# The last four rows of an output projection, summed in four rows of 256 columns or in two rows of 512

## The chip, the cores and the metric

The kernel runs on one core of one Trainium2 chip. The core has engines with an instruction stream each: TensorE (PE in the profile; its weight loads have a row of their own, PEld), VectorE (DVE), ScalarE (ACT), GpSimd (POOL) and SyncE (SP), which here only issues transfers. Sixteen DMA engines move data between device memory and the on-chip memories. The matmuls write to PSUM, everything else lives in SBUF. The metric is the device time of one execution in microseconds; of several executions the median is given.

## The reference

One token goes through two branches that share a layer norm, and both are added to the input. The attention branch uses the last 4,096 positions of the caches, 32 query heads over 4 key/value heads.

```python
xn = layernorm(x)                        # x: 1 x 1024
q = xn @ wq                              # 32 heads of 128
k, v = k_cache[-4096:], v_cache[-4096:]  # 4 heads, each serves 8 query heads
o = softmax(q @ k.T * 128 ** -0.5) @ v   # 1 x 4096
h = gelu(layernorm(xn) @ w1 + b1)        # 1 x 3584
out = x + o @ wo + h @ w2 + b2           # wo: 4096 x 1024, w2: 3584 x 1024
```

The result is one row of 1,024 numbers in bfloat16.

## The kernel before

All work is a chain of vector-matrix products, so nearly every byte that is read is used once: 4 MB each of keys, values and wq, twice 3.5 MB of w1 and of w2, and twice 4 MB of wo. The large tiles go through a ring of four SBUF buffers (`ring`, line 54); a load into a buffer has to wait until its last user is done. SP issues the loads in the order of the program: keys, wq, w1, values, w2, wo.

VectorE transposes the keys (line 186), VectorE and ScalarE spread them out (lines 200 and 202), TensorE makes q (line 238), the hidden layer (line 258), the scores (line 276) and the attention output (line 320). A few small tensors are made at the start by GpSimd: `spread` (lines 108 to 111) and `gmask` (lines 113 to 118), which are needed much later, and the two reciprocal square roots of the layer norms (lines 145 and 168). VectorE works on the layer norms meanwhile; `xc` (line 135) and `xn_f` (line 146) are two of its small steps.

The last stage is the sum over w2 and wo. `chunk_src` lists 28 rows of w2 and 32 of wo; a row is a [128, 1024] slab, and its product with one column of `hT` or `o8` gives a share of the 1,024 outputs. A matmul takes the one column as its stationary operand and up to 512 columns of the slab as its moving operand, and writes one PSUM partition. `tile_position=(0, 32 * half)` places the two halves of 512 columns in PSUM partitions 0 and 32. All rows but the last four go into the PSUM tile `accf` (line 341), which already holds x + b2.

The second wo tile is loaded in pieces of 8, 4, 2, 1 and 1 rows (line 227), so that the last rows arrive in small pieces; a matmul waits for the piece with its row. The last four rows (`TAIL = 4`) are rows 13 to 16 of that tile. They go into two PSUM tiles of their own, `acct`: the first holds columns 0 to 319 of each half and is finished by VectorE, the second columns 320 to 511, finished by ScalarE (`N1 = 320`). While the last rows arrive, `accf` is copied out to `bulk`: ScalarE copies 192 columns of both halves (line 345), VectorE 320 (line 346). ScalarE's share is added by TensorE, with the identity as stationary operand (line 353), so that ScalarE need only copy the result at the end (line 362); VectorE adds its share itself (line 361):

```python
    nc.vector.tensor_tensor(out=res[:, 0:N1], in0=acct[0][0:33, :], in1=bulk[0][:], op=ALU.add)
    nc.scalar.copy(out=res[:, N1:512], in_=acct[1][0:33, :])
    nc.sync.dma_start(out=out_v[0:1, :], in_=res[0:1, :])
    nc.scalar.dma_start(out=out_v[1:2, :], in_=res[32:33, :])
```

`res` has one half of the output in partition 0 and the other in partition 32; the partitions between are carried along. SP stores the first half and ScalarE the second, and each store needs both engines' columns.

Of the kernel before, what the change touches and what calls it, by code (L numbers as in the profile page):

```python
# [8 lines left out]
FP32 = mybir.dt.float32  # L9
BF16 = mybir.dt.bfloat16  # L10
ACT = mybir.ActivationFunctionType
ALU = mybir.AluOpType
# [4 lines left out]
def kernel(  # L17
# [14 lines left out]
    nc = tc.nc  # L32
# [21 lines left out]
    consts = ctx.enter_context(tc.tile_pool(name="consts", bufs=1))  # L54
# [8 lines left out]
    def ring_tile(name):  # L63
        return ring.tile([P, RING_ELEMS], BF16, tag="ring", name=name, align_bytes=256)
# [13 lines left out]
    for i in range(2):  # L78
        t = ring_tile(f"wq{i}")
# [8 lines left out]
    ident_f = consts.tile([P, P], FP32)  # L88
# [12 lines left out]
    with tc.issue_after(first_exp.ins):  # L101
# [8 lines left out]
    nc.gpsimd.affine_select(out=spread[:], in_=spread[:], compare_op=ALU.not_equal, fill=1.0, base=0,  # L110
                            pattern=[[-1, 4], [1, P]], channel_multiplier=-4)

    gmask = consts.tile([Hq, Hkv], FP32)
    nc.gpsimd.memset(gmask[:], 1.0)
    nc.gpsimd.affine_select(out=gmask[:], in_=gmask[:], compare_op=ALU.is_ge, fill=0.0, base=0,
# [56 lines left out]
    accf = ps_acc.tile([P, 512], FP32, tag="accf")  # L172
# [3 lines left out]
    for half in range(2):  # L176
        pr = 32 * half
        nc.tensor.matmul(accf[pr:pr + 1, :], lhsT=ones_bf[0:2, 0:1], rhs=xb2[:, 512 * half:512 * half + 512],
                         start=True, stop=False, tile_position=(0, pr))
# [24 lines left out]
    for i in range(2):  # L204
        t = ring_tile(f"w1{i}")
# [11 lines left out]
    for i in range(2):  # L217
        nr = CW2 // 2
        t = ring_tile(f"w2{i}")
# [4 lines left out]
    for i, cuts in enumerate([[0, 16], [0, 8, 12, 14, 15, 16]]):  # L224
        nr = CWO // 2
        t = ring_tile(f"wo{i}")
# [6 lines left out]
    for i, w3 in enumerate(wq_tiles):  # L233
        for r in range(4):
            c = 4 * i + r
            for j in range(NJQ):
                b, t = divmod(j, 4)
                nc.tensor.matmul(accq[32 * t:32 * t + 1, b, :], lhsT=xnT[:, c:c + 1], rhs=w3[:, r, j * 512:(j + 1) * 512],  # L238
                                 start=(c == 0), stop=(c == C - 1), tile_position=(0, 32 * t))
# [8 lines left out]
    for j in range(8):  # L248
        t, b = divmod(j, 2)
        nc.tensor.matmul(acch[32 * t:32 * t + 1, b, :NH], lhsT=ones_bf[0:1, 0:1], rhs=b1_row[:, j * NH:(j + 1) * NH],  # L250
                         start=True, stop=False, tile_position=(0, 32 * t))
    for i, w3 in enumerate(w1_tiles):
        for r in range(4):
            c = 4 * i + r
            for b in range(2):
                for t in range(4):
                    j = 2 * t + b
                    nc.tensor.matmul(acch[32 * t:32 * t + 1, b, :NH], lhsT=yT[:, c:c + 1], rhs=w3[:, r, j * NH:(j + 1) * NH],  # L258
                                     start=False, stop=(c == C - 1), tile_position=(0, 32 * t))
# [3 lines left out]
    for g in range(Hkv):  # L263
        b, th = divmod(g, 2)
# [6 lines left out]
    for a in range(WQ4 // 512):  # L271
        sp = ps_f.tile([P, 512], FP32, tag="pf", name="sp")
        for R in range(4):
            for g in range(Hkv):
                c0 = WQ4 * R + 512 * a
                nc.tensor.matmul(sp[32 * R:32 * R + 32, :], lhsT=qm[:, g, :], rhs=kT[:, g, c0:c0 + 512],  # L276
                                 start=(g == 0), stop=(g == Hkv - 1), tile_position=(0, 32 * R))
# [41 lines left out]
    for c in range(NCH):  # L319
        nc.tensor.matmul(o_all[:].rearrange("h g d -> h (g d)"), lhsT=eTb[:, 32 * c:32 * c + 32], rhs=v4[:, :, c, :],  # L320
                         start=(c == 0), stop=(c == NCH - 1))
# [11 lines left out]


    vec = {"h": lambda c: hT[:, c, 0:1], "o": lambda c: o8[:, c:c + 1]}
    N1 = 320
    TAIL = 4
    n_bulk = len(chunk_src) - TAIL
    for idx, (kind, c, wap) in enumerate(chunk_src[:n_bulk]):
        for half in range(2):  # L340
            nc.tensor.matmul(accf[32 * half:32 * half + 1, :], lhsT=vec[kind](c), rhs=wap[:, half * 512:(half + 1) * 512],  # L341
                             start=False, stop=(idx == n_bulk - 1), tile_position=(0, 32 * half))
    cols = ((0, N1), (N1, 512))
    bulk = [consts.tile([33, b - a], FP32, name=f"bulk{i}") for i, (a, b) in enumerate(cols)]
    nc.scalar.copy(out=bulk[1][:], in_=accf[0:33, N1:512])  # L345
    nc.vector.tensor_copy(out=bulk[0][:], in_=accf[0:33, 0:N1])  # L346
    acct = [ps_f.tile([P, b - a], FP32, tag="pf", name=f"acct{i}") for i, (a, b) in enumerate(cols)]
    for t in acct:
        nc.vector.memset(t[0:33, :], 0.0)
    for idx, (kind, c, wap) in enumerate(chunk_src[n_bulk:]):  # L350
        if idx == TAIL - 2:
            for half in range(2):
                nc.tensor.matmul(acct[1][32 * half:32 * half + 1, :], lhsT=ident_f[0:33, 32 * half:32 * half + 1], rhs=bulk[1][:],
                                 start=False, stop=False, tile_position=(0, 32 * half))
        for t, (n0, n1) in zip(acct, cols):
            for half in range(2):
                nc.tensor.matmul(t[32 * half:32 * half + 1, :], lhsT=vec[kind](c),  # L357
                                 rhs=wap[:, half * 512 + n0:half * 512 + n1],
                                 start=(idx == 0), stop=(idx == TAIL - 1), tile_position=(0, 32 * half))
    res = consts.tile([33, 512], BF16)  # L360
    nc.vector.tensor_tensor(out=res[:, 0:N1], in0=acct[0][0:33, :], in1=bulk[0][:], op=ALU.add)
    nc.scalar.copy(out=res[:, N1:512], in_=acct[1][0:33, :])
    out_v = out.rearrange("a b (t n) -> (a b t) n", t=2)
    nc.sync.dma_start(out=out_v[0:1, :], in_=res[0:1, :])
    nc.scalar.dma_start(out=out_v[1:2, :], in_=res[32:33, :])


# [28 lines left out]
```

## Time and profile before

| what | before |
|---|---|
| time, median of 3 runs | 101.66 us (101.6, 101.66, 101.79) |
| span of the profiled execution, first to last instruction | 100.03 us (100.0 on the page) |
| loaded from device memory | 39.86 MB, 398 GB/s over the span |
| TensorE busy | 51.2 us (51%) |
| VectorE busy | 49.7 us (50%) |
| ScalarE busy | 34.1 us (34%) |
| GpSimd busy | 3.8 us (4%) |
| mean granted TensorE clock | 0.778; 1.00 from 95 us on |

The profile shows one execution; its own whole time is not listed apart from the three runs, and 101.66 − 100.03 = 1.63 us of the median lie outside the span.

How to read its views. In the view of slices the span is cut into 40 equal parts, and each digit is the busy share of a part in tenths (9 is 90% or more). The chain that ended last is followed back from the last instruction: each step is what released the next one, or the instruction before it on its engine. A line of the timeline gives start and length in microseconds, engine, line of the code, operation, the tile written and those read, and the shape; in brackets stands how long the engine was idle before and what ended that. Neighbouring instructions of one line are merged there ("x4"), and the merged line is named after its first. The groups by form list the same operations by shape: the total busy time, then the mean of one in nanoseconds, then the idle time of the engine ahead of them. "PEq" and "SPq" are the engines' instruction sequencers.

### The profile page before, as it was taken

The page shows a single profiled execution, that of the slowest core. Times are in us where ns is not written, and L with a number is a line of the kernel's source. Part 1 is how long each engine was busy: PE and PEld are TensorE (multiplying, and loading weights), DVE is VectorE, ACT ScalarE, POOL GpSimd, SP SyncE. Part 2 cuts the span into 40 slices and gives each one's busy share as a digit, 9 for nine tenths or more (in the row PEclk, how much of TensorE's full clock was granted, in tenths as well). Part 3 has the DMA queues.
Part 4 walks back from the last instruction along what each step waited for, and adds up shares of the span by engine and source line. Part 5 has one row for each costly group of instructions (what it writes and reads, how often), then busy time and mean ns, then how long its engine had stood idle before and what let it go on. Part 6 is the DMA issues. An engine that isn't in the chain of part 4 may idle for free.

```text
span 100.0 us, 970 instructions
## 1 busy us (share of the span) xinstructions
PE 51.2 (51%) x365; PEld 20.0 (20%) x365; DVE 49.7 (50%) x92; ACT 34.1 (34%) x37; POOL 3.8 (4%) x16
## 2 busy tenths in 40 slices
PE   0065200008500940193892935999469950199980
PEld 0042200002100310031530322334123410033320
DVE  5445499999999999997125115410450000000021
ACT  5000002999999999962001044400000000000010
POOL 6005200000000000000000000000000000000000
PEclk9999999999995579555555555559985998557999
DMA  2999999999999999998999999999999999999920
GB/s 26 394 420 426 491 488 472 419 419 419 432 419 393 401 500 382 413 482 378 390 429 426 429 531 390 413 477 390 459 447 426 419 432 419 406 419 411 401 73 1
DMA packets 2878, 39.92 MB, mean 399 GB/s; under 512 B 309, under 2 KB 311, under 8 KB 698
## 3 DMA queue, kind: packets, MB, share of 16 engines
q1 hardware_dynamic: 2866, 39.85, 93.6%
q8 instruction: 3, 0.05, 0.2%
q10 hardware_dynamic: 8, 0.01, 0.0%
q14 instruction: 1, 0.01, 0.0%
HBM read 39.86 MB, written 0.00 MB: 398 GB/s over the span
## 4 chain that ended last, share of the span: by engine, by line
DVE 38%; DMA 24%; PE 21%; issue 9%; POOL 3%; ACT 2%; SPq 1%; POOLq 1%; ACTq 0%
DMA wo<-in_A_wo_dram 24%; DVE kt_scr L186 17%; DVE kT L202 16%; PE o_all L320 10%; PE sp L276 4%; PE acch L258 3%; ACT e L298 1%; DVE eTb L300 1%; PE qT_ps L262 1%; DVE m_loc L284 1%; PE acct L357 1%; SPq L229 1%; DVE q_sb L241 1%; POOLq L391 1%; POOL spread L110 1%
## 5 line engine op out<-in xcount | busy, mean ns | idle before, releaser
L200 ACT COPY kT<-kt_scr 32x1024 bf16<-32x1024 bf16 x26 | 27.1, 1042 | 14.8 <-DVE kt_scr L186 14.5
L186 DVE STREAM_TRANSPOSE kt_scr<-k_sb 128x4096 bf16<-128x4096 bf16 x4 | 17.4, 4411 | 0.0
L238 PE MATMUL accq<-wq,xnT 128*1 128x512 bf16 x64 | 7.1, 622 | 18.3 <-DMA wq<-in_A_wq_dram 18.3
L202 DVE COPY kT<-kt_scr 32x1024 bf16<-32x1024 bf16 x38 | 15.9, 419 | 0.5
L346 DVE COPY bulk<-accf 33x320 f32<-33x320 f32 x1 | 0.5, 483 | 21.9 <-ACT bulk L345 21.9
L341 PE MATMUL accf<-wo,o 128*1 128x512 bf16 x56 | 8.3, 459 | 6.0 <-DMA wo<-in_A_wo_dram 5.9
L345 ACT COPY bulk<-accf 33x192 f32<-33x192 f32 x1 | 0.3, 312 | 31.9 <-PE accf L341 31.9
L320 PE MATMUL o_all<-v_sb,eTb 128*32 128x512 bf16 x32 | 10.0, 491 | 1.0 <-DVE zcol L311 1.0
L258 PE MATMUL acch<-w,yT 128*1 128x448 bf16 x64 | 6.3, 572 | 6.0 <-DMA w<-in_B_w_dram 6.0
L341 PE MATMUL accf<-w,hT 128*1 128x512 bf16 x56 | 7.9, 451 | 0.0
L238 PEld LDWEIGHTS <-xnT 128*1 128x1 bf16 x64 | 2.1, 116 | 22.5 <-issue 22.4
L320 PEld LDWEIGHTS <-eTb 128*32 128x32 bf16 x32 | 3.8, 120 | 6.9 <-issue 3.9
L341 PEld LDWEIGHTS <-o 128*1 128x1 bf16 x56 | 2.8, 97 | 11.4 <-issue 9.2
L258 PEld LDWEIGHTS <-yT 128*1 128x1 bf16 x64 | 2.0, 115 | 9.8 <-issue 9.8
L276 PE MATMUL sp<-kT,qm 128*32 128x512 bf16 x32 | 3.8, 630 | 0.3 <-DVE qm L267 0.3
L341 PEld LDWEIGHTS <-hT 128*1 128x1 bf16 x56 | 2.7, 96 | 4.7 <-issue 2.5
L323 DVE TENSOR_TENSOR o_m<-o_all,grs 32x512 f32<-32x512 f32 x1 | 0.7, 680 | 5.8 <-PE o_all L320 5.8
L123 PE MATMUL x_ps<-ones_bf,xb 1*128 1x1 bf16 x8 | 0.7, 200 | 5.0 <-DMA xb<-in_A_x_dram 5.0
L298 ACT ACTIVATE e<-sc,nmx 128x1024 bf16<-128x1024 f32 x1 | 1.1, 1148 | 5.7 <-DVE nmx L295 5.7
L315 DVE STREAM_TRANSPOSE hT<-h_sb 128x896 bf16<-128x896 bf16 x1 | 1.7, 1706 | 2.4 <-ACT h_sb L313 2.4
L276 PEld LDWEIGHTS <-qm 128*32 128x32 bf16 x32 | 2.1, 133 | 1.4 <-issue 0.9
L281 ACT COPY sc<-sp 128x512 f32<-128x512 f32 x1 | 0.6, 585 | 4.8 <-PE sp L276 4.8
(88 smaller groups left out, 35.9 us busy)
## 6 DMA issues: line engine op xcount, KB each, us to landing
w<-in_B_w_dram SPq DMA_DIRECT2D x4, 3584.0 KB
wq<-in_A_wq_dram SPq DMA_DIRECT2D x2, 4096.0 KB, 27.0
k_sb<-in_A_k_cache_dram SPq DMA_DIRECT2D x4, 1024.0 KB, 7.1
wo<-in_A_wo_dram SPq DMA_DIRECT2D x1, 4096.0 KB, 29.4
v_sb<-in_A_v_cache_dram SPq DMA_DIRECT2D x1, 2048.0 KB, 19.2
v_sb<-in_A_v_cache_dram SPq DMA_DIRECT2D x2, 1024.0 KB, 23.1
wo<-in_A_wo_dram SPq DMA_DIRECT2D x1, 2048.0 KB
wo<-in_A_wo_dram SPq DMA_DIRECT2D x1, 1024.0 KB
```

Source lines behind the costliest of these rows:

```text
L110: nc.gpsimd.affine_select(out=spread[:], in_=spread[:], compare_op=ALU.not_equal, fill=1.0, base=0, pattern=[[-1, 4], [1, P]], channel_mul ...
L186: nc.vector.transpose(out=scr[:, g, :], in_=k2[:, g, :])
L200: nc.scalar.copy(out=dst, in_=src)
L202: nc.vector.tensor_copy(out=dst, in_=src)
L229: nc.sync.dma_start(out=tv[:, a:b, :], in_=wo_v[:, nr * i + a:nr * i + b, :])
L238: nc.tensor.matmul(accq[32 * t:32 * t + 1, b, :], lhsT=xnT[:, c:c + 1], rhs=w3[:, r, j * 512:(j + 1) * 512], start=(c == 0), stop=(c == C ...
L258: nc.tensor.matmul(acch[32 * t:32 * t + 1, b, :NH], lhsT=yT[:, c:c + 1], rhs=w3[:, r, j * NH:(j + 1) * NH], start=False, stop=(c == C - 1) ...
L276: nc.tensor.matmul(sp[32 * R:32 * R + 32, :], lhsT=qm[:, g, :], rhs=kT[:, g, c0:c0 + 512], start=(g == 0), stop=(g == Hkv - 1), tile_posit ...
L298: nc.scalar.activation(out=e128[:], in_=sc[:], func=ACT.Exp, bias=nmx[:], scale=scale, accum_out=l_loc[:])
L315: nc.vector.transpose(out=hT[:], in_=h_sb[:].rearrange("p (d c) -> p c d", c=CW2))
L320: nc.tensor.matmul(o_all[:].rearrange("h g d -> h (g d)"), lhsT=eTb[:, 32 * c:32 * c + 32], rhs=v4[:, :, c, :], start=(c == 0), stop=(c == ...
L341: nc.tensor.matmul(accf[32 * half:32 * half + 1, :], lhsT=vec[kind](c), rhs=wap[:, half * 512:(half + 1) * 512], start=False, stop=(idx == ...
```

## The change

The last four rows are summed in four PSUM rows of 256 columns, at partitions 0, 32, 64 and 96, in place of two rows of 512. `quarters` lists them: the half of the output (`half`) and the half of that half (`s`). VectorE's and ScalarE's shares become 160 and 96 columns of each quarter. Each row of wo takes eight matmuls in place of four, with half the columns each. `accf` keeps its two rows, so VectorE copies its share in two instructions, the second to partitions 64 to 96 of `bulk_a`; ScalarE copies its share in one, with the quarters behind one another in `bulk_b`. `bulk_a` is cleared once at the start by GpSimd, since VectorE's addition at the end runs over 97 partitions and not all of them are written. Each store takes two partitions with 256 numbers each.

In the order in which the instructions stand on their engines after the change, GpSimd clears `bulk_a` behind the clearing of `spread`, and its select for `spread` stands ahead of the clearing of `gmask` and of the first reciprocal square root; before, it stood behind these. On the other engines nothing changes places.

```diff
+    bulk_a = consts.tile([97, 160], FP32)
+    nc.gpsimd.memset(bulk_a[:], 0.0)
+    bulk_b = consts.tile([33, 2, 96], FP32)
...
-    N1 = 320
+    N1 = 160
+    NB = 256 - N1
...
-    cols = ((0, N1), (N1, 512))
-    bulk = [consts.tile([33, b - a], FP32, name=f"bulk{i}") for i, (a, b) in enumerate(cols)]
-    nc.scalar.copy(out=bulk[1][:], in_=accf[0:33, N1:512])
-    nc.vector.tensor_copy(out=bulk[0][:], in_=accf[0:33, 0:N1])
+    quarters = [(32 * half + 64 * s, half, s) for s in range(2) for half in range(2)]
+    accf_s = accf[0:33, :].rearrange("p (s n) -> p s n", s=2)
+    nc.scalar.copy(out=bulk_b[:], in_=accf_s[:, :, N1:256])
+    for s in range(2):
+        nc.vector.tensor_copy(out=bulk_a[64 * s:64 * s + 33, :], in_=accf_s[:, s, 0:N1])
+    cols = ((0, N1), (N1, 256))
     acct = [ps_f.tile([P, b - a], FP32, tag="pf", name=f"acct{i}") for i, (a, b) in enumerate(cols)]
     for t in acct:
-        nc.vector.memset(t[0:33, :], 0.0)
+        nc.vector.memset(t[0:97, :], 0.0)
     for idx, (kind, c, wap) in enumerate(chunk_src[n_bulk:]):
         if idx == TAIL - 2:
-            for half in range(2):
-                nc.tensor.matmul(acct[1][32 * half:32 * half + 1, :], lhsT=ident_f[0:33, 32 * half:32 * half + 1], rhs=bulk[1][:],
-                                 start=False, stop=False, tile_position=(0, 32 * half))
+            for pr, half, s in quarters:
+                nc.tensor.matmul(acct[1][pr:pr + 1, :], lhsT=ident_f[0:33, 32 * half:32 * half + 1], rhs=bulk_b[:, s, :],
+                                 start=False, stop=False, tile_position=(0, pr))
         for t, (n0, n1) in zip(acct, cols):
-            for half in range(2):
-                nc.tensor.matmul(t[32 * half:32 * half + 1, :], lhsT=vec[kind](c),
-                                 rhs=wap[:, half * 512 + n0:half * 512 + n1],
-                                 start=(idx == 0), stop=(idx == TAIL - 1), tile_position=(0, 32 * half))
-    res = consts.tile([33, 512], BF16)
-    nc.vector.tensor_tensor(out=res[:, 0:N1], in0=acct[0][0:33, :], in1=bulk[0][:], op=ALU.add)
-    nc.scalar.copy(out=res[:, N1:512], in_=acct[1][0:33, :])
-    out_v = out.rearrange("a b (t n) -> (a b t) n", t=2)
-    nc.sync.dma_start(out=out_v[0:1, :], in_=res[0:1, :])
-    nc.scalar.dma_start(out=out_v[1:2, :], in_=res[32:33, :])
+            for pr, half, s in quarters:
+                o0 = half * 512 + s * 256
+                nc.tensor.matmul(t[pr:pr + 1, :], lhsT=vec[kind](c), rhs=wap[:, o0 + n0:o0 + n1],
+                                 start=(idx == 0), stop=(idx == TAIL - 1), tile_position=(0, pr))
+    res = consts.tile([97, 256], BF16)
+    nc.vector.tensor_tensor(out=res[:, 0:N1], in0=acct[0][0:97, :], in1=bulk_a[:], op=ALU.add)
+    nc.scalar.copy(out=res[:, N1:256], in_=acct[1][0:97, :])
+    out_v = out.rearrange("a b (t s n) -> (a b t) s n", t=2, s=2)
+    nc.sync.dma_start(out=out_v[0, :, :], in_=res[0:65:64, :])
+    nc.scalar.dma_start(out=out_v[1, :, :], in_=res[32:97:64, :])
```

## The prediction

> **What bounds the kernel now.** I read the slices of the span first, then the chain that ended last, then the timeline of its last two microseconds, then the groups of instructions by form for prices.
>
> ```profile
> span 100.0 us, 970 instructions
> DVE  5445499999999999997125115410450000000021
> DMA  2999999999999999998999999999999999999920
> ```
>
> The transfers are busy from the second slice to the thirty-eighth; VectorE is idle over most of the second half. So the kernel is bound by its 39.9 MB of loads up to about 97 us, and after that by what follows the last loaded bytes. The chain shows what follows:
>
> ```profile
> 72.11 23.63 DMA wo<-in_A_wo_dram
> 95.74 0.04 issue
> 95.79 0.60 PE acct L357 x8
> 96.39 0.42 PE acct L353 x4
> 96.81 0.55 PE acct L357 x6
> 97.36 0.02 issue
> 97.38 0.48 DVE res L361
> ```
>
> Start, length, what. A piece of wo lands at 95.74, PE starts 0.04 later, and 0.48 of VectorE ends the chain. The chain steps from PE to PE between 95.79 and 97.36, but there is another wait in there. The trace's semaphore events have the sixteen completions of each load: the last ones of the pieces with rows 13 and 14, row 15 and row 16 of this wo tile come at 95.74, 96.36 and 97.00. Row 15 starts at 96.74, long after its piece (PE was late); row 16 starts at 97.04, 0.04 after its own, the same 0.04 as above, while PE could have started it at 96.95 (96.74 plus the spacings 0.135 and 0.08 below). So the last four matmuls wait for the last load, and only what comes behind 97.04 can shorten the span.
>
> ```profile
> 97.04 0.38 PE L357 MATMUL acct<-wo,o 128*1 128x320 bf16 x4
> 97.38 0.48 DVE L361 TENSOR_TENSOR res<-acct,bulk 33x320 bf16<-33x320 f32 x1 [0.93 <-PE acct L357]
> 97.46 0.31 ACT L362 CAST res<-acct 33x192 bf16<-33x192 f32 x1 [1.52 <-PE acct L357]
> 97.93 0.31 SPq L364 DMA_DIRECT2D out_dram<-res  x1
> 97.94 0.23 ACTq L365 DMA_DIRECT2D out_dram<-res  x1
> ```
>
> This is the timeline from 97.0 on: last matmuls, both halves of the result, both stores. Both stores wait for VectorE's end (97.86; ScalarE's is 97.78). Behind them lie the store and the closing handshakes, to 100.03.
>
> **The change, part by part.**
>
> *Last matmuls.* Two of 320 columns and two of 192 become four of 160 and four of 96, in four column positions. Within the last four rows, a 320-column pair is followed after 135 ns (97.040 to 97.175) and a 192-column pair after 80 ns (95.92 to 96.00): 0.42 ns per column, two matmuls at once. From the second start of a pair to PE's semaphore it takes 317 ns for 320 columns (97.043 to 97.36) and 262 ns for 192 (97.178 to 97.44), 0.43 ns per column; so 248 ns for 160 and 221 ns for 96. Four matmuls in four positions are in the trace at line 238: their first four start at 22.979, 22.983, 22.986 and 22.990, the next four 0.38 later. So the fourth starts 11 ns after the first, and VectorE's sum is ready at 97.040 + 0.011 + 0.248 = 97.30, against 97.36: −0.06. ScalarE's: four of 160 take 67 ns, so 97.118 + 0.221 = 97.34, against 97.44. The other bound is the four matmuls of line 330, in one position, whose starts lie 25 ns apart: the fourth at 97.115, done at 97.36, gain 0. I take the row with four positions and the same one-column weights, line 238.
>
> *VectorE and ScalarE.* Partitions run side by side (128x512 and 32x512 below, 692 and 680 ns), columns cost.
>
> ```profile
> L241 DVE CAST q_sb<-accq 128x512 bf16<-128x512 f32 x1 | 0.7, 692 | 0.0
> L323 DVE TENSOR_TENSOR o_m<-o_all,grs 32x512 f32<-32x512 f32 x1 | 0.7, 680 | 5.8 <-PE o_all L320 5.8
> L332 DVE CAST o<-o_ps 128x32 bf16<-128x32 f32 x1 | 0.2, 191 | 0.0
> L281 ACT COPY sc<-sp 128x512 f32<-128x512 f32 x1 | 0.6, 585 | 4.8 <-PE sp L276 4.8
> L362 ACT CAST res<-acct 33x192 bf16<-33x192 f32 x1 | 0.3, 312 | 1.5 <-PE acct L357 1.5
> ```
>
> The number before the last bar is the ns of one. VectorE: from 191 at 32 columns to 483 at 320 (line 361) it is 1.014 ns per column, so 321 at 160: −0.16. ScalarE: (585 − 312) / 320 = 0.853, so 230 at 96. Ends: VectorE 97.30 + 0.02 + 0.32 = 97.64, ScalarE 97.34 + 0.02 + 0.23 = 97.59. VectorE still comes last; its end moves by −0.22.
>
> *Stores.* Each writes two rows of 512 B from two partitions instead of one of 1 KB. The issues take 307 and 225 ns with one row, 327 to 434 with 128 rows; the two 1,024 B packets took 44 ns each. So between 0 and +0.17 (0.127 of issue, 0.044 for a second packet). Two rows are near to one: +0.01.
>
> *Hidden work.* VectorE copies the bulk sum in two instructions: 95.97 + 2 × 0.32 plus a gap is 96.65, needed at 97.32; without that 0.67 it would cost 0.18. ScalarE's copy keeps its 192 columns. Rows 13 to 16 have 32 matmuls where there were 16, each with its weight load, the identity matmuls of line 353 twice as many of half the columns. At 0.42 ns per column, four at once: 95.79 + 0.21, the 0.09 between kinds seen at 96.22 to 96.32, two passes of 0.08 (0.16 now for 192), 0.09 again: PE is ready for row 15 at 96.34 and waits until 96.41, is free at 96.52, and waits for row 16 until 97.04. That 0.52 is the cover.
>
> The two clears of acct get fewer columns, at 73.3 and 73.9, with nobody waiting. GpSimd clears bulk_a (nearest: 0.20 for 128x128, 0.51 for 32x512) and now makes `spread` ahead of its first power operation. Both fall into its idle 6.13 us before 8.50. In the kernel before that select ran beside VectorE's xn_f:
>
> ```profile
> 9.03 0.63 POOL L110 TENSOR_SCALAR_AFFINE_SELECT spread<-spread 32x512 bf16<-32x512 bf16 x1
> 9.09 0.60 DVE L146 TENSOR_SCALAR xn_f<-xc,rstd 128x8 f32<-128x8 f32 x1 [0.40 <-POOL rstd L145]
> ```
>
> xn_f took 0.60 and the like-shaped xc (line 135) 0.23, so VectorE's chain to the K transposes may come up to 0.37 sooner; the small selects that move up to that place (0.18 and 0.21) may take it back. I price either at nothing. What VectorE releases are loads, and SP issues them far ahead: the second w1 load at 29.76, while the one before it lands at 42.17; the second wo tile from 71.27, its predecessor lands at 87.23. If that cover were gone, 0.37 sooner would be 0.37 off the span. The instruction queue's three loads (at 37.1, 65.1 and 95.7 us, after 180, 423 and 698 PE records, and nobody waits) come about every 256 records; some 40 more at the end bring no fourth.
>
> *Sum.* −0.06 − 0.16 + 0.01 = −0.21. The profiled span of 100.03 becomes 99.82. The median of the runs, 101.66, lies 1.63 above the span, and I leave that alone: 101.45. By the bounds the sum runs from −0.22 to +0.01 (0 − 0.16 + 0.17).
>
> **The rivals.**
>
> *PE is bound by matmuls, not columns (slower).* Rows 13 and 14 now take 0.436 for eight, 54.5 ns each. Were this a price per matmul, they would need 16 × 0.0545 (to 96.66), 0.10, eight identity passes at 0.082 (97.42), 0.09, row 15 until 97.94; the last small matmul of row 16 would start at 98.33 and be done at 98.55, ScalarE at 98.80 against 97.86 now: +0.94, 102.6. It decides from 36 ns on: 39 starts plus 0.19 of gaps put the last start at 97.39, and then ScalarE ends at 97.86. For it: four in four positions never ran at full clock in this trace; in line 276 starts are up to 0.13 apart. Against it: starts within a group lie 4 ns apart at line 238, and at line 341 pairs of 512 columns follow each other after 213 ns, as columns would have it.
> The Trainium skill (TensorE: Matmul & The Clock Gate, section Back-to-back issue gap) speaks against the change still more: about 81 ns per matmul at 128 columns in a sustained stream of weight loads and matmuls. By that rule, by the same working, the time would be about 103.4. The trace doesn't agree: 54.5 ns at a mean of 256 columns. Of this rival's chance below it has 0.02.
>
> *Starts 25 ns apart (no change).* As at line 330: VectorE's sum is ready at 97.36, its end at 97.70, so −0.15 with the stores, 101.51. The same from stores that cost 0.02 or more. For it: the sum clears the 0.2% (0.20 us) that a measurement of this kernel tells from no change by only 0.01.
>
> *The last load lands earlier in other executions (faster still).* Now PE can't start row 16 before 96.95, then from 96.52. A piece that lands at 96.75 gains 0.16 more, 101.29; one at 96.48 gains 0.43 more, 101.02. For it: row 15 is late by 0.38 already. Against it: three runs within 0.19.
>
> **How the numbers follow.** The forecast of 101.45 has 0.47 (its own range 101.35 to 101.53), earlier landing 0.10, no change 0.28, slower 0.15. So faster 0.57, same 0.28, slower 0.15. The range starts at 101.10, which leaves out only the last fifth of what an earlier landing can bring, and ends at the sum's upper bound, 101.67, plus the 0.13 by which one run lay above the median: 101.80. Only the slower rival is outside.
>
> **What would show it.** In the changed profile the last eight matmuls start 0.04 behind the last completion, each four within some 11 ns; VectorE's last addition takes about 0.32 and starts some 0.26 after the first of them; ScalarE's cast takes 0.23 and ends before it; the stores start 0.07 after VectorE's end; PE is idle before row 16. xn_f at 0.2 to 0.4 with no change in the landing times shows the cover at the start. Matmul starts 30 ns or more apart, no idle time before row 16, a store whose completions come later after its issue, or landings that move, would make the forecast wrong.

## The result and the profile after

The changed kernel is slower: 102.33 us (median of 8 runs, 102.02 to 102.52) against 101.77 us (8 runs, 101.60 to 102.14), a ratio of 1.0045 with a 95% interval of 1.0027 to 1.0062 (this ratio, like those below, is not that of the two medians, which is 1.0055). Its profiled execution has a span of 100.43 us, against 100.03.

The view of slices of the changed kernel, its first line and the one of the transfers, says that nothing has happened to the loads:

```profile
span 100.4 us, 1012 instructions
...
DMA  3999999999999998998999998999999999999910
```

They are busy up to the same slice, and the semaphore events have the last completion of the last piece of wo at 96.98 (97.00 before). The end of the chain that ended last, of the changed kernel (start, length, what):

```profile
70.98 26.00 DMA wo<-in_A_wo_dram
96.98 0.04 issue
97.02 0.27 PE acct L364 x5
97.29 0.02 issue
97.31 0.32 DVE res L367
```

The wait for the last load, which the chain of the kernel before hid behind three steps of PE, now stands there openly: PE has nothing left to do before row 16 arrives. And the last step has 0.32 where there was 0.48. So far this is a gain. The timeline of the changed kernel from 97.0 on:

```profile
97.02 0.28 PE L364 MATMUL acct<-wo,o 128*1 128x160 bf16 x8 [0.34 <-DMA wo<-in_A_wo_dram]
...
97.31 0.32 DVE L367 TENSOR_TENSOR res<-acct,bulk_a 97x160 bf16<-97x160 f32 x1 [0.68 <-PE acct L364]
97.37 0.24 ACT L368 CAST res<-acct 97x96 bf16<-97x96 f32 x1 [1.42 <-PE acct L364]
97.70 0.61 SPq L370 DMA_DIRECT2D out_dram<-res  x1
97.71 0.57 ACTq L371 DMA_DIRECT2D out_dram<-res  x1
```

(The first line is the whole of row 16, with the 96-column matmuls behind the 160-column ones.) The last two lines are the stores' issues: 0.61 and 0.57, where they took 0.31 and 0.23. With the stores' completions from the semaphore events the whole difference can be told:

| us from the span's start | before | after | moved |
|---|---|---|---|
| last load complete | 97.00 | 96.98 | −0.02 |
| row 16 starts | 97.04 | 97.02 | −0.02 |
| VectorE done | 97.86 | 97.64 | −0.22 |
| first store starts | 97.93 | 97.70 | −0.23 |
| last store complete | 99.20 | 99.54 | +0.34 |
| span ends | 100.03 | 100.43 | +0.40 |

Everything up to the stores gains 0.23; from the first store's start to the last completion it takes 1.84 in place of 1.27, which gives back 0.56; and 0.06 comes behind, since SP checks the completions one after another and the last to arrive, ScalarE's, is now the first that it checks (before, SP's own arrived last and was checked last).

### The profile page after: what moved, and what is told of

Read it like the earlier page. It is cut to its first block, busy times and chain, and to the rows that moved or that the text cites. A ratio compares the mean times of both kernels' runs of the same rounds, so it can differ in the third digit from the quotient of the medians.

```text
span 100.4 us, 1012 instructions
## 1 busy us (share of the span) xinstructions
PE 47.8 (48%) x385; PEld 19.2 (19%) x385; DVE 49.2 (49%) x93; ACT 34.0 (34%) x37; POOL 4.0 (4%) x17
## 4 chain that ended last, share of the span: by engine, by line
DMA 81%; PE 12%; SPq 2%; issue 1%; DVE 0%
DMA wq<-in_A_wq_dram 27%; DMA wo<-in_A_wo_dram 26%; DMA v_sb<-in_A_v_cache_dram 23%; PE o_all L323 9%; DMA k_sb<-in_A_k_cache_dram 5%; PE accq L241 4%; SPq L232 2%; SPq L216 1%; DVE res L367 0%; PE acct L364 0%
## 5 line engine op out<-in xcount | busy, mean ns | idle before, releaser
L351 DVE COPY bulk_a<-accf 33x160 f32<-33x160 f32 x2 | 0.6, 316 | 24.1 <-ACT bulk_b L349 24.1
L323 PE MATMUL o_all<-v_sb,eTb 128*32 128x512 bf16 x32 | 8.6, 435 | 1.8 <-DMA v_sb<-in_A_v_cache_dram 1.8
L279 PE MATMUL sp<-kT,qm 128*32 128x512 bf16 x32 | 2.8, 496 | 0.3 <-DVE qm L270 0.3
L303 DVE STREAM_TRANSPOSE eTb<-e 128x1024 bf16<-128x1024 bf16 x1 | 1.2, 1245 | 1.4 <-ACT e L301 1.4
```

The costliest lines, as they stand in the source:

```text
L303: nc.vector.transpose(out=eTb[:], in_=e128[:])
```

## The experiments

The stores differ from those before in three ways: two rows in place of one, rows of 512 B in place of 1 KB, rows that lie 64 partitions apart. The first four kernels ask whether a store with several rows is slow by itself (theory A) or because two of them are issued at once (theory B).

**One store for both halves, on the kernel before.**

```diff
-    nc.sync.dma_start(out=out_v[0:1, :], in_=res[0:1, :])
-    nc.scalar.dma_start(out=out_v[1:2, :], in_=res[32:33, :])
+    nc.sync.dma_start(out=out_v[0:2, :], in_=res[0:33:32, :])
```

> The kernel before, with both halves of the result (partitions 0 and 32, 1 KB each) in one store from SP; ScalarE stores nothing. Theory A: a store of more than one row costs about 0.3 us more at its issue, alone or not. Then the issue takes about 0.6 (0.31 in the kernel before) and the completion comes 1.55 after its start (1.27 before), so the span is about 100.3. Theory B: the two-row stores of SP and ScalarE hold each other up. Then this one alone takes 0.3 and 1.27, and the span stays at 100.0.

The last line of this kernel's timeline:

```profile
97.88 0.61 SPq L364 DMA_DIRECT2D out_dram<-res  x1
```

Issue 0.61 and completion 1.61 after the start, with no other store beside it and rows of 1 KB. So neither a second store nor rows of 512 B are needed for the long issue: theory B by itself falls. The span is 100.4.

**Four stores of one row, on the changed kernel.**

```diff
-    nc.sync.dma_start(out=out_v[0, :, :], in_=res[0:65:64, :])
-    nc.scalar.dma_start(out=out_v[1, :, :], in_=res[32:97:64, :])
+    nc.sync.dma_start(out=out_v[0, 0:1, :], in_=res[0:1, :])
+    nc.scalar.dma_start(out=out_v[1, 0:1, :], in_=res[32:33, :])
+    nc.sync.dma_start(out=out_v[0, 1:2, :], in_=res[64:65, :])
+    nc.scalar.dma_start(out=out_v[1, 1:2, :], in_=res[96:97, :])
```

> The changed kernel, with four stores of one row of 512 B (SP: partitions 0 and 64, ScalarE: 32 and 96) in place of two stores of two rows. Theory A: each issue takes 0.22 to 0.31 again, SP's second starts at about 98.01 and completes 1.27 later at 99.28, against 99.54 in the changed kernel: span 100.1, time 0.25 under the changed kernel and level with the kernel before. Theory B: as A if the rows are what collides, but 0.3 or more later than that if two engines that issue at once are what collides, since there are now four issues. If the half-sized rows of 512 B are the cost, each single store is as slow as the two-row one, and the span is 100.4 or more.

The issues take 0.32, 0.22, 0.26 and 0.28, the last completion comes at 99.28: as theory A had it, so a row of 512 B isn't slow. But the time is not level with the kernel before: 102.04 (7 runs) against 101.82, ratio 1.003 (1.0012 to 1.0047). The second pair of issues costs more than the narrower columns save, and with four completions to check the closing takes 1.00 from the last one on, in place of 0.83. I had left the closing out.

**One store of four rows, on the changed kernel.**

```diff
-                o0 = half * 512 + s * 256
+                o0 = s * 512 + half * 256
...
-    out_v = out.rearrange("a b (t s n) -> (a b t) s n", t=2, s=2)
-    nc.sync.dma_start(out=out_v[0, :, :], in_=res[0:65:64, :])
-    nc.scalar.dma_start(out=out_v[1, :, :], in_=res[32:97:64, :])
+    out_v = out.rearrange("a b (q n) -> (a b q) n", q=4)
+    nc.sync.dma_start(out=out_v, in_=res[0:97:32, :])
```

(The sums into `accf` read their columns in the same new order.)

> The changed kernel with one store of four rows from SP in place of two stores of two (the accumulation rows take the quarters of the output in the order of their partitions, so that one store can take them; the matmuls read two runs of 256 columns instead of one of 512). Theory A with a price for each further row: issue 0.3 + 3 x 0.3 = 1.2, completion 2.2 after the start, span 100.7. Theory A with one price for more than one row: issue 0.6, completion 1.55 after the start at 97.70, span 100.1. Theory B: alone it takes 0.3 and 1.27, completes at 98.97, span 99.8, time 0.25 below the kernel before.

Issue 0.63, completion 1.66 after the start: one price for more than one row, not one for each. The span is 100.4 and not 100.1: the store starts 0.13 later than in the changed kernel (the last load came 0.08 later, and VectorE's addition another 0.05 later, behind its own second bulk copy), its completion takes 0.11 more than the 1.55 expected, and the closing 0.06 more. The time is 102.03 (10 runs), ratio 1.002 (1.0007 to 1.0034): better than the changed kernel's 1.0045, not as good as before.

**Both two-row stores on SP, on the changed kernel.** ScalarE's store becomes a second `nc.sync.dma_start`.

> The changed kernel with both two-row stores issued by SP, one behind the other. Theory A: 0.6 each, the second starts at 98.3 and completes at 99.87 or later, span 100.7. Theory B: nothing beside them, so 0.3 each, the second starts at 98.0 and completes at 99.28, span 100.1.

0.61 and 0.49, the second starts 0.66 behind the first, and completes 2.14 after the first's start: theory A. (The span of 101.1 also has a last load that came 0.44 later.) The first store takes 1.57 here, as SP's does in the changed kernel, where ScalarE's comes 0.27 behind it.

So a store of two rows costs by itself. But the loads of wo, of 128 rows each, are issued in 0.33 to 0.43. What is it about these rows?

**Neighbouring partitions, on the kernel before.** The first kernel again, with `in_=res[0:2, :]`.

> The kernel before, with one store from SP of two rows of 1 KB in neighbouring partitions, 0 and 1; partition 1 holds no result, so the second half of the output is left out. Theory A1, the 32 partitions between the rows make the two-row store slow: issue 0.31 and completion 1.27 after its start, as with one row. Theory A2, the count of rows: two is not one, issue 0.61, completion 1.6 after the start, as with partitions 0 and 32.

The last line of this kernel's timeline:

```profile
97.88 0.33 SPq L364 DMA_DIRECT2D out_dram<-res  x1
```

The same start, the same two rows of 1 KB, the same two packets, and 0.33 in place of 0.61; the completion comes 1.16 after the start in place of 1.61. It is the distance of the partitions (A1), not the count of rows (A2), on which I would have bet. The records of the transfers say where the time goes: the first packet moves 0.76 after the issue's start with neighbours and 1.21 with rows apart, and from there to the completion both take 0.40. So the whole 0.45 lies ahead of the first packet, and the 0.28 of the issue is part of it.

**Sixteen neighbouring rows, on the kernel before.** `in_=res[0:16, 0:64]`, with the output seen as sixteen rows.

> The kernel before, with one store from SP of sixteen neighbouring partitions, 64 columns each; it writes the 2 KB of the output, but not the result, which lies in two other rows. If every store of more than one row has the longer issue: 0.61 to 0.63, as with two and four rows. If only row counts between one and sixteen have it (the loads of 128 rows issue in 0.33 to 0.43): 0.33 to 0.43. If there is a small price for each row (0.609 with two rows, 0.632 with four): 0.75.

The last line of this kernel's timeline:

```profile
98.17 0.36 SPq L364 DMA_DIRECT2D out_dram<-res  x1
```

Issue 0.36, completion 1.35 after the start: with neighbours, sixteen rows cost 0.03 more at the issue than two and 0.19 more up to the completion, still less than two rows apart.

**Half of the changed kernel's stores.**

```diff
-    nc.sync.dma_start(out=out_v[0, :, :], in_=res[0:65:64, :])
-    nc.scalar.dma_start(out=out_v[1, :, :], in_=res[32:97:64, :])
+    nc.sync.dma_start(out=out_v[0, 0:1, :], in_=res[0:1, :])
+    nc.scalar.dma_start(out=out_v[1, 0:1, :], in_=res[32:33, :])
```

> The changed kernel with two stores of one row of 512 B (SP: partition 0, ScalarE: partition 32); the rows of partitions 64 and 96 are computed and not stored, so half of the output is left out. My theory, that the matmuls and the two engines give 0.22 and the shape of the stores takes it back: the stores start at 97.70, their issues take 0.31 and 0.22, the last completion comes at 98.95, span 99.8, time 0.22 below the kernel before (ratio 0.998). Rival, that the work at the end gains nothing without the profiler or that another part of the change costs time (GpSimd's clearing, the longer program): time level with the kernel before or above it.

101.67 us (12 runs) against 101.84, ratio 0.9983 (0.9969 to 0.9997): 0.17 less, and the last completion 1.26 after the first store's start. The 0.22 that the changed kernel's trace gains ahead of the stores lies within the interval, which goes from 0.03 to 0.32 us.

**The stores' shape alone, on the kernel before.**

```diff
-    nc.sync.dma_start(out=out_v[0:1, :], in_=res[0:1, :])
-    nc.scalar.dma_start(out=out_v[1:2, :], in_=res[32:33, :])
+    nc.sync.dma_start(out=out_v[0:2, 0:256], in_=res[0:33:32, 0:256])
+    nc.scalar.dma_start(out=out_v[0:2, 256:512], in_=res[0:33:32, 256:512])
```

> The kernel before, with nothing but the shape of its stores changed: SP stores columns 0 to 255 of both rows, ScalarE columns 256 to 511, two rows of 512 B each as in the changed kernel. My theory: issues of 0.61 and 0.57, last completion 1.83 after the first start in place of 1.27, so span 100.6, time 0.58 above the kernel before (ratio 1.0057). Rival, that the stores' shape is not what costs in the runs: ratio within 0.002 of 1.

The end of this kernel's timeline:

```profile
97.73 0.61 SPq L364 DMA_DIRECT2D out_dram<-res  x1
97.78 0.57 ACTq L365 DMA_DIRECT2D out_dram<-res  x1
```

102.31 us (5 runs) against 101.84, ratio 1.0042 (1.0027 to 1.0057). Issues of 0.61 and 0.57 and a last completion 1.85 after the first start, as in the changed kernel. In the runs it cost 0.47; the 0.58 that the stores lose in the trace is the upper end of the interval.

**Neighbouring partitions, on the changed kernel.** `in_=res[0:2, :]` and `in_=res[32:34, :]`.

> The changed kernel with the same two stores of two rows of 512 B, but from neighbouring partitions (SP 0 and 1, ScalarE 32 and 33); partitions 1 and 33 hold no result, so half of the output is left out. Nothing else differs. Theory, the distance: issues 0.33 and about 0.25, last completion 1.2 to 1.3 after the first start in place of 1.84, span 99.8, time 0.22 below the kernel before (ratio 0.998). Rival, that the collision of two multi-row stores is a cost of its own (ScalarE's came 0.27 behind SP's): last completion 1.5 or more after the first start, ratio 1.000 or more.

The end of this kernel's timeline:

```profile
97.86 0.32 SPq L370 DMA_DIRECT2D out_dram<-res  x1
97.87 0.25 ACTq L371 DMA_DIRECT2D out_dram<-res  x1
```

0.32 and 0.25, the last completion 1.29 after the first start. 101.71 us (12 runs) against 101.88, ratio 0.9982 (0.9967 to 0.9998). With nothing but the partitions' distance taken away the changed kernel is on the side that I forecast. And the two stores no longer hold each other up by more than two stores of one row do: 1.29 here, 1.26 with single rows, 1.84 with rows apart.

**Distance two, on the kernel before.** The first kernel with `in_=res[0:3:2, :]`.

> The kernel before with one store from SP of two rows of 1 KB in partitions 0 and 2 (partition 2 holds no result, so the second half of the output is left out). If any distance above one costs: issue 0.61, completion 1.6 after the start, as with 0 and 32. If it is the step across a group of 32 partitions: issue 0.33, completion 1.16, as with 0 and 1.

The last line of this kernel's timeline:

```profile
98.10 0.73 SPq L364 DMA_DIRECT2D out_dram<-res  x1
```

0.73, completion 1.73 after the start. Two partitions apart is no better than 32 (in this one execution it is 0.12 worse, and no run says why); it isn't a matter of groups of 32.

**A whole version with neighbours.** A matmul with a 32-column stationary operand, of which only the last column isn't zero, puts its sum into the last partition of its group of 32, and the next group's first partition is its neighbour.

```diff
+    o8p = consts.tile([P, 4, 32], BF16)
+    sel0 = consts.tile([33, 32], FP32)
...
-    quarters = [(32 * half + 64 * s, half, s) for s in range(2) for half in range(2)]
+    quarters = [(64 * half + 32 * s, half, s) for half in range(2) for s in range(2)]
+    pick = {0: (sel0[:], ident_f[0:33, 0:1]), 1: (ident_f[0:33, 1:33], ident_f[0:33, 32:33])}
...
-                nc.tensor.matmul(t[pr:pr + 1, :], lhsT=vec[kind](c), rhs=wap[:, o0 + n0:o0 + n1],
+                m = 1 if s else 32
+                nc.tensor.matmul(t[pr:pr + m, :], lhsT=vec[kind](c) if s else o8p[:, idx, :], rhs=wap[:, o0 + n0:o0 + n1],
...
-    nc.vector.tensor_tensor(out=res[:, 0:N1], in0=acct[0][0:97, :], in1=bulk_a[:], op=ALU.add)
+    nc.vector.tensor_copy(out=res[:, 0:N1], in_=acct[0][0:97, :])
...
+    nc.sync.dma_start(out=out_v[0, :, :], in_=res[31:33, :])
+    nc.scalar.dma_start(out=out_v[1, :, :], in_=res[95:97, :])
```

`o8p` is cleared and gets the last four columns of `o8` in its column 31; `sel0` is zero but for a one in row 0, column 31. Both shares of the bulk sum are added by identity matmuls, VectorE's ahead of row 16.

> A version that computes the reference with the four rows of the changed kernel, but with the two quarters of each half in neighbouring partitions: 31 and 32 for the first half, 95 and 96 for the second. For 31 and 95 the stationary operand gets 32 columns, the last one o8's and the others zero; the bulk sum comes in through identity matmuls for VectorE's share too, ahead of row 16, and VectorE only copies at the end. My theory, the distance of the partitions is the price: issues of about 0.33, completion 1.2 to 1.3 after the first start at 97.70, span 99.8, time 0.22 below the kernel before (ratio 0.998) and 0.7 below the changed kernel. Rival, two multi-row stores at once collide whatever their partitions: last completion 0.3 or more later, time level with the kernel before or above. A third: the eight fp32 matmul passes ahead of row 16 come too late for it (PE not ready at 97.0), which would show as row 16 starting more than 0.04 after its load.

Level: 101.91 us (12 runs) against 101.88, ratio 1.0006 (0.9993 to 1.0019). The stores are as hoped (0.33 and 0.26, last completion 1.32 after the first start), and the sign of the third guess is there: row 16 starts late. From this kernel's PE timeline:

```profile
96.91 0.44 PE L366 MATMUL acct<-bulk_a,ident_f 33*1 33x160 f32 x5
...
97.30 0.24 PE L372 MATMUL acct<-wo,o8p 128*32 128x160 bf16 x1
```

The last load is complete at 96.92, but VectorE's identity passes run until about 97.2, and row 16 starts at 97.30. Not all of this need be the version's: in this execution ScalarE's bulk copy, for which PE waited, came at 95.93, 0.30 later than in the kernel before (the last section says what goes with that). How much of the 0.39 that row 16 is late belongs to the passes, this profile doesn't separate.

**The same, with the last eight rows in the four-row sum.** `TAIL = 8`, and both identity additions between rows 14 and 15.

> The version with neighbouring partitions (31 and 32, 95 and 96) again, but with the last eight rows of wo in the four-row sum in place of four, so that the bulk sum is copied out after row 8 and both identity additions stand between rows 14 and 15. It computes the reference. My theory, that only the late identity passes (row 16 started 0.39 behind its load) kept the first version level: row 16 starts within 0.05 of its last load, completion 1.2 to 1.3 after the first store's start, span 99.8, time 0.2 below the kernel before (ratio 0.998) and 0.65 below the changed kernel. Rival, the 32-column stationary operands and the wider sums cost as much as the narrower columns save: row 16 late again by 0.2 or more, ratio 1.000.

The end of the chain of this kernel, and the end of its timeline:

```profile
96.72 0.22 PE acct L372 x6
96.94 0.02 issue
96.96 0.27 PE acct L372 x5
97.23 0.02 issue
97.26 0.33 DVE res L375
```

```profile
97.65 0.33 SPq L378 DMA_DIRECT2D out_dram<-res  x1
97.66 0.26 ACTq L379 DMA_DIRECT2D out_dram<-res  x1
```

Row 16 starts 0.04 behind its load (complete at 96.92), VectorE is done at 97.58, and the last completion comes 1.32 after the first store's start. 101.67 us (12 runs) against 101.89, ratio 0.9984 (0.9971 to 0.9997), and below the changed kernel's 1.0045: it beats both kernels, the one before by about 0.2 us (0.03 to 0.30 by the interval). That the late passes are what kept the first version level is likely and not shown: the clock returned to full earlier in this profile (90.86 against 92.30), and the intervals of the two ratios overlap a little.

## Why the prediction was wrong

*The step that failed* is the price of the stores, +0.01 within bounds of 0 and +0.17. It was +0.56, and +0.06 behind them. I took the number of rows as what differs and bounded it by the loads of 128 rows. All those rows lie in neighbouring partitions, and nothing in the trace of before had rows apart; the bound looked like one from both sides and had no row for the property that mattered. It wasn't even the trace's bound for 128 rows: 0.33 to 0.43 is what the loads of wo take, but in the same trace one load of keys took 0.70 to issue and one of values 1.22. The runs show the parts of the price: rows apart cost 0.45 up to the completion, 0.28 of it at the issue (0.33 and 1.16 against 0.61 and 1.61, the same rows on the same queue), and two such stores at once another 0.2 to 0.3 (1.57 and 1.61 for one, 1.84 and 1.85 for two). (These don't add up to the 0.56, since they start from one store's 1.16 and not from the 1.27 of two stores with one row each.) With the same two stores on the same kernel, the distance alone makes 1.84 out of 1.29. Why a distance costs what it does stays open.

*The other steps held in the profile of the changed kernel.* The four matmuls of row 16 start at 97.023, 97.026, 97.029 and 97.033, within the 11 ns forecast and not 25 ns apart; VectorE's addition takes 0.324 (0.321 forecast), ScalarE's cast 0.239 (0.230); VectorE's end moves by −0.22, as in the sum. The cover at PE is there: the last matmuls of row 15 start at 96.48 and row 16 waits until 97.02.

*The work at the start stayed hidden.* GpSimd's select moved, and xn_f took 0.23 in place of 0.60, as the timeline of the changed kernel has it (GpSimd, VectorE):

```profile
2.48 0.63 POOL L110 TENSOR_SCALAR_AFFINE_SELECT spread<-spread 32x512 bf16<-32x512 bf16 x1
...
9.18 0.23 DVE L149 TENSOR_SCALAR xn_f<-xc,rstd 128x8 f32<-128x8 f32 x1 [0.40 <-POOL rstd L148]
```

The K transposes start at 12.04 in place of 12.32, and the last load still lands within 0.02 of where it did. The instruction queue again makes three loads.

*The cover at the end is not always there*, which the prediction, worked out from one execution, didn't say. In the profile of the changed kernel with two single stores, the last load is complete at 96.93, and yet (VectorE, then PE):

```profile
97.04 0.32 DVE L351 COPY bulk_a<-accf 33x160 f32<-33x160 f32 x1
97.11 0.28 PE L364 MATMUL acct<-wo,o 128*1 128x160 bf16 x8
97.46 0.32 DVE L367 TENSOR_TENSOR res<-acct,bulk_a 97x160 bf16<-97x160 f32 x1
```

ScalarE's bulk copy came at 96.37 there, 0.73 later than in the changed kernel's own profile. Row 16 starts 0.18 behind its load, since PE is late, and VectorE's second bulk copy ends 0.10 before its addition starts. The kernel before meets the same: in the execution with sixteen rows its row 16 starts 0.32 behind its load.

*The slower rival* ended on the right side for a wrong reason. PE is not bound by its number of matmuls: rows 13 and 14 start their four groups at 95.807, 95.875, 95.917 and 95.985, 42 to 68 ns for each four, 10 to 17 ns for one. The 81 ns for each matmul of 128 columns in a sustained stream that the Trainium skill gives (TensorE: Matmul & The Clock Gate, section Back-to-back issue gap) don't hold for these matmuls of 96 and 160 columns in four column positions. *The rival of an earlier last load* has little for it: the earliest last completion in any profile here is 96.84, and in that execution, of the kernel before with other stores, PE was in time all the same: row 16 started at 96.88, 0.04 behind its load. The prediction's 96.95, before which PE could not start row 16, holds for one execution.

*The range* ended at 101.80, from an upper bound that was no bound. The chances came from the same bound: the slower side had 0.15, all of it on PE, and none on the stores.

## What to carry to other kernels

A last store pays its whole way from issue to completion on the path, so its access pattern must be priced like any instruction: one row, or rows in neighbouring partitions, but not rows with partitions between. Where results come out of matmuls at partitions 0, 32, 64 and 96, zero columns in the stationary operand can bring two of them side by side. And when a bound is taken from the nearest row, ask in which property that row is near: here a load of 128 rows was near in count and far in layout. A cover that is read from one execution holds for that execution.

## What the runs showed of the hardware

A transfer of two rows from partitions 0 and 1 was issued in 0.33 us, from 0 and 2 in 0.73, from 0 and 32 in 0.61; four rows 32 apart took 0.63 and sixteen neighbours 0.36. All of these are stores issued by SP, one execution each. The Trainium skill (DMA: Bandwidth & Descriptors, section Issuing engines are not separate DMA queues) calls the time to initiate a transfer usually small relative to the transfer; here it is 0.61 of 1.61 us.

The granted clock returned to full at 91.11 in the profile of the kernel before, at 90.96 in the changed kernel's and at 92.30 in the first version with neighbours, where ScalarE's bulk copy then came at 95.93 in place of 95.63. The other profiles with a four-row tail go the same way, but for the one whose last load came 0.44 late: a return by 91.9 goes with a bulk copy at 95.50 to 95.75, a return at 92.3 to 93.1 with one at 95.93 to 96.37. Row 16 starts more than 0.04 behind its load in the second group alone, in three of its six profiles. The granted clock changes in multiples of 3.41 us. The Trainium skill (TensorE: Matmul & The Clock Gate, section Part 1: The HAM clock gate) has a window of that length that runs freely and isn't reset by a kernel's start; the records agree. The runs of one kernel spread by 0.5 us; a late return goes with a row 16 that starts 0.18, 0.32 and 0.39 behind its load in three profiles, but how much of the spread comes from that isn't shown.
